# Three fixed buffers in place of a ring of three, earlier weight differences, and a third engine for sixteen weight products

## The chip, the cores and the metric

The kernel runs on one core of one Trainium2 chip. The metric is the device time of one execution in microseconds (us). The engines are named as the profile names them: PE (TensorE, matrix products), DVE (VectorE), ACT (ScalarE), POOL (GpSimd) and SP (SyncE). PSUM is the memory that PE writes its results to, SBUF the memory that the other operands lie in.

## What is computed

Sliding-window attention with four sink positions over 4 batches, 8 heads, 768 positions and head size 64, and behind it a layer norm and an MLP with a ReLU and a residual sum:

```
keep   = (key position < 4) or (0 <= query - key < 128)
a      = softmax(q k^T / 8 where keep, else -1e9)
x      = a v, heads side by side: (4, 768, 512)
xn     = (x - mean) / sqrt(var + 1e-6) * g_ln
out    = x + relu(xn @ w_ch1) @ w_ch2        # w_ch1 512 x 2048, w_ch2 2048 x 512
```

Inputs and output are float32; matrix operands are bfloat16.

## The kernel before

The 3072 rows are worked in 12 chunks c of 256 rows, two tiles t of 128 rows each; three chunks make a batch. Each chunk has an attention part (`attend_tile` for chunks 0 and 1, `attend` after them): scores on PE (L732), their exponentials on ACT (L746), a product with the mask on DVE (L750), and the product with v on PE (L769, L774). `value` then makes the row of x on DVE (L787 reciprocal, L789 x, L793 and L795 the norm's statistics), 1/sqrt(var) on POOL (L801, L802) and the centred row xc on DVE (L804). Each chunk has an MLP part (`mlp`): eight products with w1 (named ph, L839 for chunks 0 and 1 and L846 after them), eight ReLUs (named rl, L856 on ACT or L858 on DVE), and the product with w2. For chunks 0 and 1 that second product is the plain one (L877, L885). From chunk 2 on it is Strassen's (Winograd's form): `wino` makes sums of the hidden blocks (s1 to s4, L909, DVE) and seven products (p1 to p7, L926), some of them with four differences of blocks of w2, t1 to t4, which are made once (the lines named w2t, L997). DVE adds the results (L940, L947).

The norm's gain g_ln is folded into the activations for chunks 0 to 2. For chunk 3 and later it is multiplied into w1 once, in place: sixteen products of 128x512 with a column of g_ln (named w1g, L987 to L990). The four that belong to one quarter of w1 can start when chunk 2 has made its last use of that quarter, and chunk 3 needs them.

Nothing is ordered by hand. Every operation is entered with the engines it may run on and their planned costs (time on the engine, time to the result), what it depends on, and a priority. `Plan.run` lays them out in planned time: an operation takes the engine that would end it first, and of those that could start within a quarter of a microsecond, the one with the lowest priority number goes first. PE operations of priority 40 and more keep strict priority order. The resulting order is what each engine's queue gets, and each engine then works through its queue in that order.

The first q and k rows (chunk 0's first tile, as float32) and the q and k of chunks 1, 2 and 3 come through a ring `n4` of three buffers; after them the buffers are used for t1, t2 and t3, and t4 has a tile of its own. The loads of w2 are POOL DMAs (L523).

```
    ring("n4", 3, [128, H, 4, 64], BF16)
    n4_b = [Buf(f"n4_{c}", "n4") for c in range(1, PAR["by_dma"])]
    idle = [o for z in n4_b for o in z.users]
```

`idle` holds every user of the buffers of chunks 1, 2 and 3, and each of the sixteen differences waits for all of them.

Of the kernel before, what the change touches and what calls it, by code (L numbers as in the profile page):

```python
# [7 lines left out]
FP32 = mybir.dt.float32  # L8
BF16 = mybir.dt.bfloat16
# [192 lines left out]
def act(n):  # L202
    t = 0.065 + 0.000833 * n
    return (t, t + 0.105)
# [7 lines left out]
def fix(occ, extra=0.09):  # L212
    return (occ, occ + extra)
# [4 lines left out]
SW_4 = (1.4, 0.7, 0.9)  # L218
# [10 lines left out]
PAR = dict(strict=40.0, win=0.4, tr=-8.0, sc=-5.3, sc1=-2.0, av=2.0, trx=9.0, by_dma=4, x_by_dma=3,  # L229
           w1p=(1.6, 2.6, 2.7, 2.8), pm=2, w2p=(4.5, 4.51, 4.52, 4.53), by_tile=2, wino=2, vp=(0.0, 0.1, 2.0, 2.1, 4.2, 4.3), ld1=0.05)  # L230


def general(tc, nc, slots, pairs, ones, ident_f, ident, w1, w2, mhalf, g_s, g_r, q, k, v, out, scale):


    V, A, G, T, DMA = nc.vector, nc.scalar, nc.gpsimd, nc.tensor, nc.gpsimd.dma_start
    B, H, S, D = q.shape
    RB, HP, NS, DM = S // 128, H // 2, g_s.shape[2], H * D
    f32 = {n: [t.bitcast(FP32) for t in slots[n]] for n in ("kq", "n4", "kts", "pe")}
    flat = lambda t: t.rearrange("p a b -> p (a b)")  # L240
    half = [t.rearrange("p a k b -> p (a k b)")[:, 512 * i:512 * i + 512] for t in f32["kq"] for i in range(2)]
    q_n, k_n, v_n = half[0], half[1], half[2:4]
    qT, kT0, kT1 = [t.rearrange("p (a b) -> p a b", a=HP) for t in half[4:7]]
    kT, ksT = [kT0, kT1], f32["kts"][0]
    ks_n, vs_n = flat(f32["pe"][6]), flat(f32["pe"][7])
    sc = [f32["n4"][i].rearrange("p h i d -> p (h i d)").rearrange("p (h c) -> p h c", h=4) for i in range(2)]
    aT = [[flat(f32["pe"][2 * i + a]) for a in range(2)] for i in range(3)]
    xs, os_, xn, xnt = slots["ot"][0:2], slots["ot"][2:4], slots["xc"][0], slots["xnt"][0]
    h1 = [slots["hq"][u // 4][:, u % 4, :] for u in range(8)]
# [7 lines left out]
    with tc.For_i(0, B, 1) as b:  # L257
# [5 lines left out]
        for r in range(RB):  # L263
            x, cur, prev = xs[r % 2], r % 2, (r + 1) % 2
# [67 lines left out]
            st = slots["st"][r % 2]  # L332
# [5 lines left out]
            pb = ones[0].bitcast(BF16)  # L338
# [23 lines left out]
def kernel(  # L362
# [12 lines left out]
    nc = tc.nc  # L375

    B, H, S, D = q.shape
# [17 lines left out]
    P = Plan()  # L395

    def ring(name, n, shape, dtype, pool=consts):
        P.ring(name, [Slot(pool.tile(shape, dtype, name=f"{name}{i}"), f"{name}{i}") for i in range(n)])
# [3 lines left out]
    ones = [psum.tile([128, 512], FP32, name=f"one{i}") for i in range(4)]  # L402
    P.ring("pair", [Slot(pairs[i], f"pair{i}", banks[2 * i:2 * i + 2]) for i in range(2)])
    P.ring("one", [Slot(ones[i], f"one{i}", [banks[4 + i]]) for i in range(4)])
    ring("n4", 3, [128, H, 4, 64], BF16)
    ring("nat", 8, [128, H, 64], BF16)
    ring("vn", 7, [128, H, 65], BF16)
    ring("kq", 4, [128, HP, 2, 256], BF16)
# [12 lines left out]
    def const(name, shape, dtype):  # L421
        return consts.tile(shape, dtype, name=name)

    ident_f, ident = const("ident_f", [128, 128], FP32), const("ident", [128, 128], BF16)
# [7 lines left out]
    w1 = [const(f"w1_{c}", [128, NDM, 512], BF16) for c in range(4)]  # L432
    w2 = [const(f"w2_{c}", [128, 4, DM], BF16) for c in range(4)]
    w2t = [t.rearrange("p (c s n) -> p c s n", c=4, s=2) for t in (
        *[z.tile.rearrange("p h i d -> p (h i d)") for z in P.rings["n4"]], const("w2t", [128, 2048], BF16))]
    junk = const("junk", [128, 512], BF16)
    rec, low = const("rec", [128, NT, H], FP32), const("low", [128, NT, H], FP32)
    n_bad, flag = const("n_bad", [128, 1], FP32), const("flag", [1, 1], mybir.dt.int32)
# [9 lines left out]
    Bw2t = [[Buf(f"w2t{i}_{c}") for c in range(4)] for i in range(4)]  # L448
# [4 lines left out]
    V, G = nc.vector, nc.gpsimd  # L453
# [35 lines left out]
    def negs(e):  # L489
# [15 lines left out]
         writes=[Bc["gt"]], dma=HW_T)  # L505
    for h in range(H):
        p0 = 32 * (h // 2) + NS * (h % 2)
# [14 lines left out]
    for c in range(4):  # L522
        P.op(f"w2ld{c}", {"POOL": (0.75, 0.8)}, PAR["w2p"][c], lambda e, c=c: G.dma_start(  # L523
            w2[c], moe_w_ch2[512 * c:512 * (c + 1), :].rearrange("(t p) n -> p t n", p=128)),
            writes=[Bw2[c]], dma=SW_W)
# [7 lines left out]
    xnt_t = [Buf(f"xnt_t{t}") for t in range(NT)]  # L533

    tile_of, scores = {}, {}
    n4_b = [Buf(f"n4_{c}", "n4") for c in range(1, PAR["by_dma"])]

    def early(t):
        return 0.5 + 0.8 * t
# [22 lines left out]
    def load4(c, nm, prio, loaded):  # L562
        b, R = c // RC, c % RC
        p0 = 64 * "kq".index(nm)
        ap = (k if nm == "k" else q)[b, :, 256 * R:256 * R + 256, :].rearrange("h (p i) d -> p h (i d)", i=4)
        P.op(f"{nm}ld{c}", {"POOL": (0.72, 0.75)}, prio, lambda e: G.dma_start(
            n4_b[c - 1].t[p0:p0 + 64].rearrange("p h i d -> p h (i d)"), ap), writes=[loaded, n4_b[c - 1]], dma=SW_4)

    def chunk(c):
        b, R = c // RC, c % RC  # L570
        d = at(c, "tr") if c >= 2 else early(2 * c)
        ld = d - 14.0 if c >= RC else 4.0
        T = Buf(f"kq{c}", "kq")
        kq_b[c] = T
        if c == 0:
            f0, c0 = Buf("f0", "n4"), Buf("c0", "hq")
            raw = lambda: f0.t.rearrange("p h i d -> p (h i d)").bitcast(FP32).rearrange("p (h i d) -> p h i d", h=H, i=2)
            cut = lambda: c0.t.rearrange("p a b -> p (a b)")[:, 0:1024].rearrange("p (i h d) -> p i h d", i=2, h=H)
            for x, src in enumerate((k, q)):
                ap = src[b, :, 0:128, :].rearrange("h (p i) d -> p h (i d)", i=2)  # L580
# [4 lines left out]
            for x, (nm, src) in enumerate((("k", k), ("q", q))):  # L585
                nat.append(Buf(f"{nm}n01", "nat"))
                ap = src[b, :, 128:256, :].rearrange("h p d -> p h d")
                P.op(f"{nm}ld01", {"POOL": (0.87, 0.9)}, -50 + 0.1 * x, lambda e, nat=nat[x], ap=ap: G.dma_start(nat.t, ap),  # L588
                     writes=[nat[x]], dma=SW)
            for t in range(2):  # L590
                for hh in range(2):
                    hs = slice(4 * hh, 4 * hh + 4)
                    pt, done, half = Buf(f"pt0{t}{hh}", "one"), Buf(f"T0{t}{hh}"), Buf(f"c0{hh}")
# [6 lines left out]
                    def tr(e, pt=pt, t=t, hh=hh):  # L600
                        pb = pt.t.bitcast(BF16)[:, 0:512]
                        for h in range(2):
# [7 lines left out]
                         hold=[T] + ([] if t else [c0]), writes=[pt])  # L610
# [5 lines left out]
        elif c < PAR["by_dma"]:  # L616
            loaded = Buf(f"l{c}")
            for i in range(2):
                load4(c, "kq"[i], (PAR["ld1"] if c == 1 else ld) + 0.01 * i, loaded)
            for hh in range(2):  # L620
                pt = Buf(f"pt{c}{hh}", "one")

                def tr(e, pt=pt, hh=hh):
                    pb = pt.t.bitcast(BF16).rearrange("p (h k i g) -> p h i k g", h=2, k=2, i=4)
                    for h in range(2):
                        for i in range(4):
                            for h2 in range(2):
                                nc.tensor.transpose(pb[64 * h2:64 * h2 + 64, h, i], n4_b[c - 1].t[:, 4 * hh + 2 * h + h2, i, :], ident)  # L628
                P.op(f"tr{c}{hh}", pe(0.46), d + 0.02 + 0.1 * hh, tr, reads=[loaded, Bc["ident"]],
                                  hold=[n4_b[c - 1], T], writes=[pt], mode="c")  # L630
                done = Buf(f"T{c}{hh}")
                tile_of[2 * c, hh] = tile_of[2 * c + 1, hh] = done
                evict(f"ev{c}{hh}", d + 0.05 + 0.1 * hh, 1024,
                      lambda pt=pt: pt.t.bitcast(BF16).rearrange("p (m i g) -> p m g i", m=4, i=4),
                      lambda hh=hh: T.t[:, 2 * hh:2 * hh + 2].rearrange("p h k (g i) -> p (h k) g i", i=4), [pt], [T, done], fp=True)
        else:
            for x, (nm, src) in enumerate((("k", k), ("q", q))):
                for i in range(2):
                    nat = Buf(f"{nm}n{c}{i}", "nat")
                    ap = src[b, :, 256 * R + 128 * i:256 * R + 128 * (i + 1), :].rearrange("h p d -> p h d")  # L640
                    P.op(f"{nm}ld{c}{i}", {"POOL": (0.87, 0.9)}, ld + 0.01 * i + 0.1 * x,
                         lambda e, nat=nat, ap=ap: G.dma_start(nat.t, ap), writes=[nat], dma=SW, after=behind(c))  # L642
                    P.op(f"tr{nm}{c}{i}", {"SP": (1.2, 1.2)}, d + 0.01 * i, lambda e, nat=nat, i=i, x=x: dma_t(
                        T.t[:, :, x, 128 * i:128 * i + 128], nat.t.rearrange("p h d -> p (h d)")),
                        reads=[nat], writes=[T], dma=HW_X, after=[scores[c - 1]])
        if R == 0:
            kts = Buf(f"kts{b}", "kts")
# [334 lines left out]
    for c in range(NC):  # L982
        mlp(c)
        if c == PAR["x_by_dma"] - 1:
            for s in range(4):
                for j in range(NDM):
                    P.op(f"w1g{s}{j}", {"DVE": fix(0.36), "ACT": act(512)}, 16.0 * c + 11.0 + 2 * s + 0.1 * j,  # L987
                         lambda e, s=s, j=j: (V.tensor_scalar_mul if e == "DVE" else nc.scalar.mul)(  # L988
                             w1[s][:, j, :], w1[s][:, j, :], gt[:, j:j + 1]),
                         reads=[Bw1[s], Bc["gt"]], writes=[Bw1g[s]], after=last_use[s])  # L990

    idle = [o for z in n4_b for o in z.users]
    for qt in range(4):
        b11, b12, b21, b22 = (w2[qt][:, 2 * i:2 * i + 2, 256 * j:256 * j + 256] for i in range(2) for j in range(2))
        t1, t2, t3, t4 = (w2t[i][:, qt] for i in range(4))
        for i, (o, x0, x1) in enumerate(((t1, b12, b11), (t2, b22, t1), (t3, b22, b12), (t4, b21, t2))):
            P.op(f"w2t{i}_{qt}", {"DVE": dve(512, 0.52)}, 16.0 * PAR["wino"] - 6.0 + qt + 0.1 * i, lambda e, o=o, x0=x0, x1=x1: V.tensor_tensor(  # L997
                o, x0, x1, op=ALU.subtract), reads=[Bw2[qt]] + ([Bw2t[i - 1][qt]] if i in (1,) else [Bw2t[1][qt]] if i == 3 else []),
                writes=[Bw2t[i][qt]], after=idle)

    def guard(e):
        V.tensor_scalar(low, rec, LOW, HIGH, op0=ALU.max, op1=ALU.min)
# [12 lines left out]
    t, was = 1.3, "n"  # L1015
    for o in order:
# [7 lines left out]
        if free and left > 0.11:  # L1024
            i, nth = min(free)[1], 0
# [6 lines left out]
        t, was = o.start + o.engs["PE"][0], o.mode_out  # L1032
# [6 lines left out]
                o.emit(o.eng)  # L1039
    bad = nc.values_load(flag, min_val=0, max_val=128 * NT * H)  # L1040
    with tc.If(bad > 0):
        slots = {n: [s.tile for s in P.rings[n]] for n in ("kq", "kts", "n4", "pe", "ot", "xc", "xnt", "hq", "st")}
        general(tc, nc, slots, pairs, ones, ident_f, ident, w1, w2, mhalf, g_s, g_r, q, k, v, out, scale)
    global LAST
    LAST = P
# [35 lines left out]
```

## Time and profile before

| | us |
|---|---|
| median of 3 runs | 217.86 (217.83 to 217.99) |
| profiled execution, its own time | 217.35 |
| its span in the trace | 215.9 |
| PE busy, matmuls | 206.2 (96%) |
| DVE busy | 159.9 (74%) |
| ACT busy | 118.1 (55%) |
| POOL busy | 84.1 (39%) |
| granted TensorE clock, mean | 0.998 |

A profile row names the line, the engine, the operation, output and input by their names in the program with the buffer number left out (so n4, kq or w2t appear as n, kq or w2t, and w1 and w2 both as w). A stretch "idle before" an instruction is put down to whatever released it last. The end of a matmul is modelled, so that consecutive matmul groups overlap a little in the timeline.

### The profile page before, as it was taken

How to read it: one execution, taken by the hardware profiler on the slowest of the kernel's cores; microseconds unless marked ns; L12 is line 12 of the kernel's file. 1: busy time of each engine (PE TensorE's matmuls, PEld its weight loads, DVE VectorE, ACT ScalarE, POOL GpSimd, SP SyncE). 2: the span in 40 equal slices, each digit the busy share in tenths (PEclk: the TensorE clock that was granted, in tenths of full speed). 3: DMA queues.
4: the chain of work that ended last, by engine and by line, in shares of the span. 5: the costliest groups of instructions: out<-in, count | busy, mean ns of one | idle time of the engine just before them, and what ended most of it. 6: DMA issues, size and time to landing. Idle time of an engine off the chain costs nothing.

```text
span 215.9 us, 5921 instructions
## 1 busy us (share of the span) xinstructions
PE 206.2 (96%) x2381; PEld 168.5 (78%) x2387; DVE 159.9 (74%) x402; ACT 118.1 (55%) x182; POOL 84.1 (39%) x126
## 2 busy tenths in 40 slices
PE   6989999999998999999999999999999999999990
PEld 2568995684785897897987987988988988988880
DVE  5499644598898689699687796797786787794470
ACT  2578567166799655554556456455456456432600
POOL 7968574487057048048066075075110110110000
PEclk9999999999999999999999999999999999999999
DMA  6999999999929949949949959929942520222003
GB/s 109 169 185 207 193 197 206 179 203 157 191 51 136 155 100 110 164 123 114 179 100 148 195 56 150 210 34 155 170 104 37 149 49 0 100 49 99 2 3 109
DMA packets 100146, 27.23 MB, mean 126 GB/s; under 512 B 88848, under 2 KB 97040, under 8 KB 100112
## 3 DMA queue, kind: packets, MB, share of 16 engines
q0 software_dynamic: 67712, 13.37, 79.3%
q1 hardware_dynamic: 31872, 13.15, 31.5%
q8 instruction: 20, 0.33, 0.6%
q10 hardware_dynamic: 528, 0.26, 0.5%
q14 instruction: 14, 0.11, 0.2%
HBM read 27.30 MB, written 6.29 MB: 156 GB/s over the span
## 4 chain that ended last, share of the span: by engine, by line
PE 81%; ACT 6%; POOL 4%; DMA 3%; DVE 1%; issue 1%; DVEq 0%; ACTq 0%; POOLq 0%
PE one L846 30%; PE one L926 27%; PE one L839 6%; PE one L877 5%; PE pair L732 4%; PE pair L774 4%; ACT w L988 4%; DMA n<-in_q_dram 3%; PE pair L769 2%; POOL nat L642 2%; PE one L628 1%; POOL nat L588 1%; ACT pe L746 1%; ACT hq L856 1%; PE one L812 1%
## 5 line engine op out<-in xcount | busy, mean ns | idle before, releaser
L856 ACT ACTIVATE hq<-one 128x512 bf16<-128x512 f32 x93 | 55.5, 597 | 56.6 <-PE one L846 44.6
L846 PE MATMUL one<-xnt,w 128*128 128x256 bf16 x640 | 74.4, 273 | 0.0
L846 PEld LDWEIGHTS <-w 128*128 128x128 bf16 x640 | 61.4, 98 | 7.1
L746 ACT ACTIVATE pe<-pair 128x1024 bf16<-128x1024 f32 (+1 forms) x40 | 36.3, 957 | 22.4 <-PE pair L732 21.0
L801 POOL TENSOR_SCALAR st<-st 128x1 f32<-128x1 f32 x24 | 6.6, 274 | 92.6 <-DVE rec L787 77.0
L926 PEld LDWEIGHTS <-hs 128*128 128x128 bf16 x320 | 30.0, 98 | 5.6 <-issue 1.3
L926 PE MATMUL one<-n,hs 128*128 128x256 bf16 x240 | 29.6, 273 | 0.0
L750 DVE TENSOR_TENSOR pe<-pe,mask 128x1024 bf16<-128x1024 bf16 (+1 forms) x40 | 24.9, 644 | 5.0 <-ACT pe L746 4.9
L940 DVE TENSOR_TENSOR tm<-one,x 128x256 f32<-128x256 f32 x40 | 16.8, 421 | 12.2 <-PE one L926 12.1
L926 PEld LDWEIGHTS <-hq 128*128 128x128 bf16 x240 | 23.3, 98 | 3.0 <-ACT hq L856 0.3
L553 POOL DMA_DIRECT2D vn<-in_v_dram x24 | 21.7, 922 | 3.0 <-PE one L877 0.9
L926 PE MATMUL one<-w,hq 128*128 128x256 bf16 x160 | 19.3, 273 | 0.0
L909 DVE TENSOR_TENSOR hs<-hq 128x512 bf16<-128x512 bf16 x40 | 15.4, 413 | 5.1 <-ACT hq L856 5.1
L947 DVE TENSOR_TENSOR ot<-one,tm 128x256 f32<-128x256 f32 x40 | 16.7, 417 | 1.3 <-PE one L926 1.1
L789 DVE TENSOR_TENSOR x<-pair,rec 128x512 bf16<-128x512 f32 x24 | 16.6, 691 | 0.8
L793 DVE BATCH_NORM_STATS2 st<-x 128x6 f32<-128x512 bf16 x24 | 16.6, 690 | 0.4
L839 PE MATMUL one<-xnt,w 128*128 128x128 bf16 x256 | 16.0, 219 | 0.0
L642 POOL DMA_DIRECT2D nat<-in_k_dram x16 | 14.9, 931 | 2.7 <-DMA w<-in_moe_w_ch_dram 2.7
L642 POOL DMA_DIRECT2D nat<-in_q_dram x16 | 14.2, 904 | 3.4 <-DMA w<-in_moe_w_ch_dram 3.4
L802 POOL TENSOR_TENSOR st<-st,mhalf 128x1 f32<-128x1 f32 x24 | 14.7, 612 | 2.0
L877 PE MATMUL one<-w,hq 128*128 128x512 bf16 x60 | 15.0, 380 | 0.2
L839 PEld LDWEIGHTS <-w 128*128 128x128 bf16 x256 | 14.6, 98 | 0.7
(94 smaller groups left out, 234.6 us busy)
## 6 DMA issues: line engine op xcount, KB each, us to landing
out_dram<-ot SPq DMA_DIRECT2D x24, 256.0 KB
w<-in_moe_w_ch_dram POOLq DMA_DIRECT2D x8, 512.0 KB, 13.3
vn<-in_v_dram POOLq DMA_DIRECT2D x24, 128.0 KB, 7.2
nat<-in_k_dram POOLq DMA_DIRECT2D x17, 128.0 KB, 5.4
nat<-in_q_dram POOLq DMA_DIRECT2D x17, 128.0 KB, 6.6
n<-in_k_dram POOLq DMA_DIRECT2D x3, 256.0 KB, 13.5
n<-in_q_dram POOLq DMA_DIRECT2D x3, 256.0 KB, 14.5
kq<-nat SPq DMA_TRANSPOSE x32
```

The costliest lines, as they stand in the source:

```text
L553: P.op(f"vld{t}", {"POOL": (0.87, 0.9)}, prio, lambda e: G.dma_start(bv.t[:, :, 0:64], v[b, :, 128 * r:128 * (r + 1), :].rearrange("h p d ...
L642: lambda e, nat=nat, ap=ap: G.dma_start(nat.t, ap), writes=[nat], dma=SW, after=behind(c))
L746: P.op(f"ex{c}{hp}", {"ACT": act(2 * n)}, d + 0.1 + 0.05 * j, lambda e, pp=pp, pb=pb: nc.scalar.activation(pb.t[:, :, 0:n], pp.t[:, :, 0:n ...
L750: V.tensor_mul(pb.t[:, :, 0:n], pb.t[:, :, 0:n], mm),
L789: P.op(f"x{t}", {"DVE": dve(512)}, d + 0.11, lambda e: V.tensor_tensor(x.t.rearrange("p (a h c) -> p a h c", a=2, c=64), pv()[:, :, :, 0:6 ...
L839: nc.tensor.matmul(ph.t[:, 128 * s:128 * s + 128], lhsT=w1[u // 2][:, j, 128 * s:128 * s + 128], rhs=xnt.t[:, j, 128 * (u % 2):128 * (u % ...
L846: nc.tensor.matmul(ph.t[:, 256 * s:256 * s + 256], lhsT=w1[ht // 4][:, j, 128 * (ht % 4):128 * (ht % 4 + 1)], rhs=xnt.t[:, j, :], start=j ...
L856: nc.scalar.activation(hg.t[:, u % 4, :], ph.t, AF.Relu)
L877: nc.tensor.matmul(pc.t[:, 0:wd], lhsT=(hq[s // 2].t[:, (2 * s + i) % 4, 128 * ii:128 * ii + 128] if by_tile else hq[ht // 8].t[:, ht // 2 ...
L926: nc.tensor.matmul(at(r), lhsT=get(left, g)[:, v, s, :], rhs=rhs, start=first and n == 0, stop=n == 7, skip_group_check=True)
L940: return P.op(f"tm{name}_{c}", {"DVE": dve(256, 1.14)}, pr, lambda e: V.tensor_tensor(tm[name].t, at(r), xs[i].t[:, sl], op=ALU.add), read ...
L947: return P.op(f"o{c}_{half}", {"DVE": dve(256, 1.14)}, pr, lambda e: V.tensor_tensor(ots[i].t[:, sl], at(r), tm[name].t, op=ALU.add), read ...
```

## The change

There are three parts. The ring of three becomes three rings of one buffer, n4a, n4b, n4c, and the loads are tied to them: chunks 0 and 3 in n4a, chunk 1 in n4b, chunk 2 in n4c. The first load, a buffer of its own name before, is the first of the same list. Second, each of the four differences waits only for the users of the buffer that it is written to: t1 goes to n4b, t2 to n4c, t3 to n4a, and t4, in its own tile, waits for no buffer. Third, the sixteen products of w1 with the gain may also run on POOL, at a planned 0.9 us on the engine and 1.0 us to the result, and their planned cost on ACT goes from 0.49 and 0.60 us to 0.61 and 0.72 us.

```diff
-    ring("n4", 3, [128, H, 4, 64], BF16)
+    for i in range(3):
+        ring(f"n4{'abc'[i]}", 1, [128, H, 4, 64], BF16)
...
-        *[z.tile.rearrange("p h i d -> p (h i d)") for z in P.rings["n4"]], const("w2t", [128, 2048], BF16))]
+        *[P.rings[f"n4{x}"][0].tile.rearrange("p h i d -> p (h i d)") for x in "bca"], const("w2t", [128, 2048], BF16))]
...
-    n4_b = [Buf(f"n4_{c}", "n4") for c in range(1, PAR["by_dma"])]
+    n4_b = [Buf(f"n4_{c}", f"n4{'abca'[c]}") for c in range(PAR["by_dma"])]
...
-            n4_b[c - 1].t[p0:p0 + 64].rearrange("p h i d -> p h (i d)"), ap), writes=[loaded, n4_b[c - 1]], dma=SW_4)
+            n4_b[c].t[p0:p0 + 64].rearrange("p h i d -> p h (i d)"), ap), writes=[loaded, n4_b[c]], dma=SW_4)
...
-            f0, c0 = Buf("f0", "n4"), Buf("c0", "hq")
+            f0, c0 = n4_b[0], Buf("c0", "hq")
...
-                    P.op(f"w1g{s}{j}", {"DVE": fix(0.36), "ACT": act(512)}, 16.0 * c + 11.0 + 2 * s + 0.1 * j,
-                         lambda e, s=s, j=j: (V.tensor_scalar_mul if e == "DVE" else nc.scalar.mul)(
+                    P.op(f"w1g{s}{j}", {"DVE": fix(0.36), "ACT": (0.61, 0.72), "POOL": (0.9, 1.0)}, 16.0 * c + 11.0 + 2 * s + 0.1 * j,
+                         lambda e, s=s, j=j: (nc.scalar.mul if e == "ACT" else V.tensor_scalar_mul if e == "DVE" else G.tensor_scalar_mul)(
...
-    idle = [o for z in n4_b for o in z.users]
+    idle = [[o for z in n4_b if z.ring == f"n4{x}" for o in z.users] for x in "bca"] + [[]]
...
-                writes=[Bw2t[i][qt]], after=idle)
+                writes=[Bw2t[i][qt]], after=idle[i])
```

The remaining lines of the diff give the same three buffers their new names where the general path (L233, run only if a softmax sum is out of bounds) uses them.

More of the change, by code (lines that the diff above doesn't have):

```diff
@@ L238, in general @@
     RB, HP, NS, DM = S // 128, H // 2, g_s.shape[2], H * D
-    f32 = {n: [t.bitcast(FP32) for t in slots[n]] for n in ("kq", "n4", "kts", "pe")}
+    f32 = {n: [t.bitcast(FP32) for t in slots[n]] for n in ("kq", "n4a", "n4b", "kts", "pe")}
     flat = lambda t: t.rearrange("p a b -> p (a b)")
@@ L245, in general @@
     ks_n, vs_n = flat(f32["pe"][6]), flat(f32["pe"][7])
-    sc = [f32["n4"][i].rearrange("p h i d -> p (h i d)").rearrange("p (h c) -> p h c", h=4) for i in range(2)]
+    sc = [f32[("n4a", "n4b")[i]][0].rearrange("p h i d -> p (h i d)").rearrange("p (h c) -> p h c", h=4) for i in range(2)]
     aT = [[flat(f32["pe"][2 * i + a]) for a in range(2)] for i in range(3)]
@@ L627, in tr @@
                             for h2 in range(2):
-                                nc.tensor.transpose(pb[64 * h2:64 * h2 + 64, h, i], n4_b[c - 1].t[:, 4 * hh + 2 * h + h2, i, :], ident)
+                                nc.tensor.transpose(pb[64 * h2:64 * h2 + 64, h, i], n4_b[c].t[:, 4 * hh + 2 * h + h2, i, :], ident)
                 P.op(f"tr{c}{hh}", pe(0.46), d + 0.02 + 0.1 * hh, tr, reads=[loaded, Bc["ident"]],
-                                  hold=[n4_b[c - 1], T], writes=[pt], mode="c")
+                                  hold=[n4_b[c], T], writes=[pt], mode="c")
                 done = Buf(f"T{c}{hh}")
@@ L1041 @@
     with tc.If(bad > 0):
-        slots = {n: [s.tile for s in P.rings[n]] for n in ("kq", "kts", "n4", "pe", "ot", "xc", "xnt", "hq", "st")}
+        slots = {n: [s.tile for s in P.rings[n]] for n in ("kq", "kts", "n4a", "n4b", "pe", "ot", "xc", "xnt", "hq", "st")}
         general(tc, nc, slots, pairs, ones, ident_f, ident, w1, w2, mhalf, g_s, g_r, q, k, v, out, scale)
```

## The prediction

> **What bounds the kernel now.** The summary by engine comes first: PE is busy 206.2 of 215.9 us, and the row of granted clock is 9 in every slice, so a change of DVE, ACT and POOL work can move the end only where PE stands still for it. In the view by slices, PE stands at 9 from 16 us on in all slices but that of 64.8 to 70.2 us and the last. Next, busy time by stretches, for the MLP of chunk 2 (its ph products, then its Strassen products with the scores of chunk 4 among them) and, as a control, the same two stages of chunk 5, which issue the same PE work and have no w1g products:
>
> ```profile
> 55.44:63.17 7.73, 7.73 (x89) 7.00 (x88) 6.92 (x16) 6.38 (x12) 1.43 (x4) 1.00 0.75 139
> 63.17:72.47 9.30, 8.07 (x87) 6.23 (x85) 7.46 (x21) 9.25 (x14) 5.63 (x7) 1.00 1.45 111
> 104.12:111.85 7.73, 7.73 (x91) 6.99 (x89) 6.06 (x16) 4.18 (x7) 2.03 (x5) 1.00 1.65 163
> 111.85:119.50 7.65, 7.65 (x87) 6.18 (x85) 5.93 (x17) 4.69 (x6) 4.99 (x6) 1.00 1.49 122
> ```
>
> The columns are the stretch, its length, and the busy time of PE, PE's weight loads, DVE, ACT and POOL. The first stage is equally long in both chunks. The second takes 9.30 us against 7.65: **1.65 us lost**, with ACT busy for 9.25 of it. The chain that ended last says with what:
>
> ```profile
> 64.84 0.84 ACT w L988 x2
> 65.68 0.20 issue
> 65.89 0.02 ACTq L754
> 65.90 0.05 issue
> 65.96 1.95 ACT w L988 x3
> 67.91 0.91 ACT pe L746
> 68.81 0.61 ACT w L988
> 69.42 0.92 ACT pe L746
> 70.34 0.04 issue
> 70.38 0.40 PE pair L732 x6
> ```
>
> The w1g products (L988) stand before the exponentials (L746) of chunk 4, and PE cannot write its second half of scores until an exponential empties a pair of PSUM banks. The timeline and the waits show the loss at PE:
>
> ```profile
> 70.38 0.23 PE L732 MATMUL pair<-kq,kq 64*128 64x128 bf16 x2 [1.12 <-ACT pe L746]
> PEld L926 <- ACT hq L856: 0.3, 1, 0.3
> ```
>
> That is 1.12 us there and 0.3 us where p2 waits for the last ReLU; the other 0.2 us are smaller gaps. The differences of w2 lie elsewhere: sixteen L997, starting between 46.87 and 53.21 us. PE in 44 to 56 us is busy 3.95, 3.89 and 3.95 of 4 us each, so it loses 0.21 us there in all.
>
> **The change, part by part.** *Buffers.* In the ring, three loads take the three buffers, and the fourth (chunk 3, issued at 27.68) can take the first load's, which its casts at 6.7 us had freed long before. That is the new assignment too. No operation is added or removed, and POOL's and SP's DMAs stay as they were: 0.
>
> *Differences.* t1, t2 and t4 no longer wait for chunk 3's transposes (L628, 45.69 to 46.7), only for the w2 quarter and for transposes that ended by 30.4. POOL's queue shows when w2 lands, since its DMAs wait for it:
>
> ```profile
> 32.53 0.88 POOL L642 DMA_DIRECT2D nat<-in_k_dram  x1 [1.29 <-DMA w<-in_moe_w_ch_dram]
> 34.81 0.87 POOL L642 DMA_DIRECT2D nat<-in_k_dram  x1 [1.40 <-DMA w<-in_moe_w_ch_dram]
> 37.35 0.87 POOL L642 DMA_DIRECT2D nat<-in_q_dram  x1 [1.67 <-DMA w<-in_moe_w_ch_dram]
> 39.95 0.87 POOL L642 DMA_DIRECT2D nat<-in_q_dram  x1 [1.72 <-DMA w<-in_moe_w_ch_dram]
> ```
>
> L997 starts every 0.37 us (0.33 to 0.45), so three differences per landing are 1.1 us, twelve 4.4 us. DVE is busy 5.11 us of 30 to 40 and 2.28 of 40 to 44, so 6.6 us are free. The first thing behind them on DVE's in-order queue is the mask product of chunk 2 (last one 38.17 to 38.86); PE reads it at 40.89, which leaves 2.0 us. So three differences ahead of it, and a landing that comes up to 0.9 us after its planned place, cost nothing; beyond that PE pays one for one. The last three end about 41.1, before the reciprocal at 41.58. What leaves 46.87 to 53.2 frees DVE where PE lost 0.21 us. Bounds: 0.2 us gained, 0.5 us lost if PE's order (free below priority 40) comes out worse. I take 0, the nearest row being PE's own 99%.
>
> *Products.* Before, 14 ran on ACT, two on DVE. ACT's 14 start 0.61 us apart when back to back (five in 64.73 to 67.9). The planner gives POOL a product whenever ACT is booked more than 0.28 us ahead (1.0 less 0.72). POOL is free from 57.2 to about 65.3 but for two 1/sqrt pairs (0.83 us planned, 0.87 measured): (8.1 - 1.7)/0.9 = 7 products. So 7 on POOL, 7 on ACT, two on DVE. ACT sheds 7 x 0.61 = 4.3 us. Its last ReLU then ends near 63.95, two products follow until 65.2, and the control puts the first exponential 2.27 us after the ph products, here at 65.44: in time. The 1.12 us stall goes, with the small gaps. Of p2's 0.3 us I keep 0.2, since the control has the ReLU end exactly when p2 starts, and a product may stand half in the way. ACT's gain: 1.65 - 0.2 = 1.45 us.
>
> What a POOL product takes no row shows. Below: a 128x1 TENSOR_SCALAR takes 0.22 us, a 128x128 select 0.29, hence 0.22 + 511 x 0.07/127 = 0.50. Above: the dearest fixed cost, 0.57 (L802, 128x1), plus ACT's 0.72 for the same product, 1.3. I take 0.9, the middle. The Trainium skill (GPSIMD Engine Reference, Performance versus the Vector engine) has 769 ns for 512 elements in a tight loop; no run here shows it, and seven by that are 0.9 us less on POOL, with the sum unchanged.
>
> **What speaks against it** is a row from the start of the kernel, where both engines read SBUF at once:
>
> ```profile
> 18.93 0.68 DVE L692 TENSOR_TENSOR pe<-pe,mask 128x1024 bf16<-128x1024 bf16 x1
> 18.97 1.07 POOL L802 TENSOR_TENSOR st<-st,mhalf 128x1 f32<-128x1 f32 x1
> ```
>
> L802 takes 0.57 us alone and 1.07 here: it waited out DVE's instruction. L801 likewise goes from 0.22 to 0.37 beside an xc (L804). Nothing here shows DVE waiting for POOL, because POOL's instructions are short and DVE waits for their results anyway. The Trainium skill (SBUF — State Buffer, SBUF: two separate sides) says that the port pair is an exclusive lock for the whole instruction, whichever engine starts first, for DVE instructions with two SBUF inputs or a two-port mode. The trace agrees for POOL waiting (0.5 us); by the rule for both directions the gain would be 0.45 (217.4), with POOL alone waiting 1.45 (216.4).
>
> The mechanism, from rows: POOL goes from each 1/sqrt pair straight to a product, and DVE's xc (L804, behind that pair) and its eight sums (L909) come into up to five products. If each holds DVE for half its length, that is 5 x 0.45 = 2.25 us; if for all, 4.5; if DVE does not wait, 0. In the control the sum that p6 needs ends at 114.09 and p6 starts at 115.33: 1.24 us of slack. PE would thus lose 0, 1.0 or 3.3 us of its 1.45. I take 0.5, between none and the half.
>
> Sum: 1.45 - 0.5 = 0.95, with 0 from the differences. Against the profiled execution: span 215.9 - 0.95 = 214.95, plus the 1.45 us outside the span (217.35 - 215.9), 216.4. That execution was 0.5 us under the median of the runs, so **216.9** against the median 217.86.
>
> **The rivals.** (1) *DVE is held up by POOL and becomes the bound, slower.* Place: p7 and p6 of chunk 2. It decides from 1.24 + 1.45 = 2.7 us of DVE delay; at 3.6 (0.72 per meeting) it is 217.86 + 0.9 = 218.8, at the full 4.5 219.7. For it: DVE is busy 6.92 and 7.46 us in the two stages, 2.4 more than in the control, and the row above. Against: two L858 ReLUs (0.68 each) and two L988 (0.34) make up 2.0 of that 2.4 and can go to a lighter ACT. A POOL product of 1.3 us or more leads to the same place, the xc behind it coming late. (2) *The gain is eaten, no change:* the same, with 2.2 to 3.1 us of delay (1.45 us less a stall within 0.44 of it), 217.4 to 218.3. (3) *The planner gives POOL few products*, since ACT and DVE end each sooner: with three, ACT sheds 1.8 us, enough for the 1.12 us stall alone, and 3 x 0.45 us of DVE delay cost 0.1: 216.8, inside the forecast. (4) *A difference blocks DVE while its w2 quarter is under way*, and chunk 2's attention is late: with more than 2.0 us of it PE loses the excess; 1 us more gives 217.9 after the gain.
>
> **How the numbers follow.** About 0.2% (0.44 us) can be told from no change. Gain of more than that, by the forecast or (3): 0.58, spanning 216.2 (1.65 us, all of it) to 217.4. Rival (2) 0.14 and (4) 0.05 give no change: 0.19. Rival (1) 0.18, and PE's order worse by more than 0.5 us in 32 to 56 us 0.05: slower, 0.23. The range goes from 216.1 to 218.6; under it 0.05, over it 0.10. The forecast's own range is 216.2 to 217.4.
>
> **What would show it.** Right: L997 twelve times between 32 and 42 us and four times after 46.7; about seven POOL rows L988 of 0.5 to 1.3 us between 57 and 66; the second stage of chunk 2 at 7.7 to 8.6 us instead of 9.30; no PE wait for an L746 there. Wrong: PE waiting for L909 at p7 or p6, L804 or L909 starting late behind an L988 of POOL, a stage of 9.3 us or more, or PE under 3.85 of 4 us anywhere in 32 to 56.

## The result and the profile after

The changed kernel takes 218.63 us (median of 16 runs, 217.9 to 219.74) against 217.85 us before (16 runs, 217.07 to 218.34): a ratio of 1.0047, 95% interval 1.0031 to 1.0063. The medians differ by 0.78 us and the means by 1.03; the interval of the ratio spans 0.7 to 1.4 us. The kernel is slower by about half a per cent, where the forecast was 0.95 us faster, with a chance of 0.23 for slower. The median lies 0.03 us above the predicted range.

The profiled execution of the changed kernel took 219.26 us, span 217.8. That is 1.9 us more than the profiled execution of before, and not all of it is the change. Line numbers are one higher than before from the ring's definition on. The program is the same up to the first landing of w2, yet PE reaches chunk 1's transposes (L629) at 13.46 us here and at 12.68 before, because chunk 1's q rows landed later. Over all the profiles below that moment lies anywhere from 12.09 to 13.62 us, whatever the kernel. That would account for the spread of the times of one kernel, more than a microsecond (it is not shown, as each kernel has one profile). It is the reason why stages are compared below and not ends.

Three stages tell the change. Their limits are PE's first instruction of each: chunk 3's transposes, chunk 2's first ph product, its product p1, chunk 3's first ph product. Busy time by these stretches, with the columns as in the prediction (length, then PE, weight loads, DVE, ACT, POOL); the first row is the first stage before, the other three are the changed kernel's:

```profile
45.69:55.44 9.75, 9.53 (x88) 4.80 (x89) 8.95 (x26) 7.70 (x15) 6.70 (x9) 1.00 2.37 183
...
46.56:56.96 10.40, 9.63 (x90) 4.79 (x89) 6.95 (x19) 7.70 (x15) 6.81 (x9) 1.00 1.84 183
56.96:64.69 7.73, 7.73 (x89) 6.99 (x88) 5.49 (x11) 6.22 (x11) 5.87 (x6) 1.00 0.55 100
64.69:74.44 9.75, 8.16 (x86) 5.99 (x84) 8.15 (x23) 7.81 (x12) 7.33 (x9) 1.00 1.15 103
```

Before, the first of them took 9.75 us, the second 7.73, the third 9.30 (the prediction shows the rows of these two). So there are **two separate losses, 0.65 us in the first stage and 0.45 us in the third**, 1.10 us together. All other stages agree within 0.1 us. The timelines show who waited in the first stage, before (two lines) and in the changed kernel:

```profile
49.55 0.47 POOL L801 TENSOR_SCALAR st<-st 128x1 f32<-128x1 f32 x1
...
51.21 0.40 PE L812 MATMUL one<-ident,xc 128*128 128x128 bf16 x4
...
48.67 0.63 POOL L802 TENSOR_SCALAR st<-st 128x1 f32<-128x1 f32 x1
49.39 0.57 POOL L803 TENSOR_TENSOR st<-st,mhalf 128x1 f32<-128x1 f32 x1
...
49.99 0.41 DVE L805 TENSOR_SCALAR xc<-x,st 128x512 bf16<-128x512 bf16 x1 [0.77 <-POOL st L803]
...
50.46 0.40 PE L813 MATMUL one<-ident,xc 128*128 128x128 bf16 x4 [0.77 <-DVE xc L805]
```

PE stands for 0.77 us before the transposes of tile 5, waiting for DVE's xc, which waits for POOL's 1/sqrt; before, it didn't wait there. And in the third, again first two lines of before, the xc of the two tiles:

```profile
60.53 0.41 DVE L804 TENSOR_SCALAR xc<-x,st 128x512 bf16<-128x512 bf16 x1 [0.19 <-POOL st L802]
63.44 0.41 DVE L804 TENSOR_SCALAR xc<-x,st 128x512 bf16<-128x512 bf16 x1 [0.17 <-POOL st L802]
...
58.66 3.14 POOL L989 TENSOR_SCALAR w<-w,gt 128x512 bf16<-128x512 bf16 x2 [5.13 <-PE one L847]
61.88 0.22 POOL L802 TENSOR_SCALAR st<-st 128x1 f32<-128x1 f32 x1
62.76 3.11 POOL L989 TENSOR_SCALAR w<-w,gt 128x512 bf16<-128x512 bf16 x2
65.95 0.22 POOL L802 TENSOR_SCALAR st<-st 128x1 f32<-128x1 f32 x1
...
62.79 0.79 DVE L805 TENSOR_SCALAR xc<-x,st 128x512 bf16<-128x512 bf16 x1 [0.93 <-POOL st L803]
66.86 0.41 DVE L805 TENSOR_SCALAR xc<-x,st 128x512 bf16<-128x512 bf16 x1 [0.95 <-POOL st L803]
...
65.97 1.26 PE L927 MATMUL one<-w,hq 128*128 128x256 bf16 x10 [0.46 <-DVE hq L859]
69.25 0.61 PE L927 MATMUL one<-n4a,hs 128*128 128x256 bf16 x4 [0.71 <-DVE hs L910]
71.17 1.03 PE L927 MATMUL one<-w2t,hq 128*128 128x256 bf16 x8 [0.43 <-DVE tm L941]
```

A w1g product takes POOL 1.57 us. Four of them, two ahead of each 1/sqrt pair, make each xc wait almost a microsecond (0.19 and 0.17 before), everything behind xc on DVE is late, and PE waits for DVE three times. The 1.12 us wait for ACT's exponential is gone, as forecast; the waits for DVE are more.

### The profile page after: what moved, and what is told of

It reads as the page before. It is cut to its first block, busy times and chain, and to the rows that moved or that the text cites. A ratio compares the mean times of both kernels' runs of the same rounds, so it can differ in the third digit from the quotient of the medians.

```text
span 217.8 us, 5925 instructions
## 1 busy us (share of the span) xinstructions
PE 206.8 (95%) x2387; PEld 168.0 (77%) x2387; DVE 161.1 (74%) x401; ACT 116.6 (54%) x179; POOL 90.0 (41%) x130
## 4 chain that ended last, share of the span: by engine, by line
PE 79%; DVE 9%; POOL 4%; DMA 4%; issue 1%; DVEq 0%; POOLq 0%
PE one L847 30%; PE one L927 27%; PE one L878 6%; PE one L840 5%; PE pair L733 4%; PE pair L775 4%; DMA n4b<-in_q_dram 4%; DVE st L794 2%; PE pair L770 1%; DVE x L790 1%; DVE hs L910 1%; POOL st L803 1%; PE one L629 1%; POOL nat L589 1%; POOL nat L643 1%
## 5 line engine op out<-in xcount | busy, mean ns | idle before, releaser
L878 PE MATMUL one<-w,hq 128*128 128x512 bf16 x64 | 15.3, 380 | 0.0
L803 POOL TENSOR_TENSOR st<-st,mhalf 128x1 f32<-128x1 f32 x24 | 14.2, 591 | 2.0
L805 DVE TENSOR_SCALAR xc<-x,st 128x512 bf16<-128x512 bf16 x24 | 10.2, 425 | 6.3 <-POOL st L803 6.2
```

The costliest lines, as they stand in the source:

```text
L878: nc.tensor.matmul(pc.t[:, 0:wd], lhsT=(hq[s // 2].t[:, (2 * s + i) % 4, 128 * ii:128 * ii + 128] if by_tile else hq[ht // 8].t[:, ht // 2 ...
```

## The experiments

The first two runs take the parts of the change one by one, the next two take the first loss apart. Lengths are those of the three stages, in order, from one profile each.

**The early differences alone.** The third part of the change is undone:

```diff
-    {"DVE": fix(0.36), "ACT": (0.61, 0.72), "POOL": (0.9, 1.0)}
+    {"DVE": fix(0.36), "ACT": act(512)}
```

> The changed kernel without its third part: the sixteen w1g products keep the costs and engines of before, the differences of w2 stay early. Theory: the change loses in two separate places, and this kernel has the first alone. From chunk 3's transposes to chunk 2's first ph product PE takes 10.4 us as in the changed kernel (9.75 before), because PE's queue has the transposes of tile 5 earlier than xc can deliver them; the second Strassen stage of chunk 2 takes 9.3 us as before. Together 217.85 + 0.65 = 218.5. Rival: the early differences cost nothing, all the loss comes from POOL's products: 9.75 and 9.3 us, 217.85.

Measured: 10.41, 7.73 and 9.30 us; 218.19 against 217.57, ratio 1.0032 (1.0015 to 1.0049). The first loss is that of the differences alone, with the same 0.77 us wait.

**POOL's share alone.**

```diff
-                writes=[Bw2t[i][qt]], after=idle[i])
+                writes=[Bw2t[i][qt]], after=[o for z in idle for o in z])
```

> The changed kernel with all sixteen differences waiting for all three buffers again, as before; POOL keeps its share of the w1g products. Theory: only the second place is left. 9.75 us from chunk 3's transposes to the first ph product, then 9.7 us for the Strassen stage of chunk 2, since POOL's products of 1.57 us stand ahead of its 1/sqrt pairs and DVE's xc waits: 217.85 + 0.45 = 218.3. Rival (the stage is worse only because the earlier loss shifts it, and POOL's share helps by itself): 8.5 us and 217.0.

Measured: 9.76, 7.73 and 9.76 us; 218.06 against 217.57, ratio 1.0021 (1.0006 to 1.0036). The second loss is that of POOL's share alone. By stages the two losses add up to the change's.

**The place of tile 5's transposes in PE's queue.**

```diff
-             hold=[xnt_b[c]])
+             hold=[xnt_b[c]], nb=49.6 if t == 5 else 0.0)
```

> The changed kernel, with the transposes of tile 5 not planned before 49.6 us, so that PE's queue has them behind one more product with w2, where they stood before. Everything else, the early differences too, stays. Theory: the first loss is the place of these transposes in PE's queue, so PE takes 9.75 us there again, and only the second loss is left: 218.3. Rival: the loss is DVE being late with the differences or with xc whatever PE's order: 10.2 us or more, 218.7 or more.

Measured: 9.47, 7.72 and 9.75 us; 217.65 against 217.57, ratio 1.0002 (0.9983 to 1.0022). With PE's order of before, the early differences lose nothing; they gain 0.28 us, more than the 0.21 us that the prediction had counted as PE's idle time there, and more than the theory said. So the place of the transposes in PE's queue makes the first loss. How they came there can be read from the queues. Of DVE's sixteen differences nine are made between 33 and 42 us, and only one is left in front of tile 5's aggregate (L796), where six were. It starts 1.50 us after the start of chunk 3's transposes (3.43 before). The planner puts the 1/sqrt pair after two of POOL's four loads instead of after all four, and then places the transposes of tile 5 in PE's queue four matmuls L878 behind those of tile 4, where before twelve and eight matmuls of chunk 3's scores lay between. On the chip xc comes later than these transposes' turn, and PE, in order, stands still.

**Why xc is later than planned.** In the kernel with the early differences alone, the three differences that DVE makes back to back at that moment are left out, with every order kept:

```diff
-    lambda e, o=o, x0=x0, x1=x1: V.tensor_tensor(
+    lambda e, o=o, x0=x0, x1=x1, out=(i, qt) in ((2, 1), (2, 2), (0, 3)): None if out else V.tensor_tensor(
```

> The kernel with the early differences alone (w1g as before), and the three differences that DVE makes back to back while POOL makes tile 5's 1/sqrt left out (t3 of quarters 1 and 2, t1 of quarter 3 keep what lay there). Orders as planned with them. Theory: those three hold POOL's first instruction of the pair back, so it drops from 0.63 to 0.22 us, xc comes 0.4 us sooner, PE's wait before tile 5's transposes falls from 0.77 to about 0.35 us and the stage from chunk 3's transposes to the first ph product from 10.4 to 10.0 us. Rival (POOL is late only by its DMA issues): 0.77 and 10.4 us stay.

Measured: 10.00, 7.72 and 9.30 us (one execution). The timeline of this kernel:

```profile
46.47 1.86 POOL L643 DMA_DIRECT2D nat<-in_k_dram  x2
48.41 0.22 POOL L802 TENSOR_SCALAR st<-st 128x1 f32<-128x1 f32 x1
...
49.78 0.40 PE L813 MATMUL one<-ident,xc 128*128 128x128 bf16 x4 [0.35 <-DVE xc L805]
```

POOL's first instruction takes 0.22 instead of 0.63 us and PE's wait drops from 0.77 to 0.35, both as expected. So 0.4 us of the wait is POOL held back by DVE's differences. The rest has no run of its own, but the row of POOL's two loads fits it: the aggregate was done at 47.98 us, the loads that stand ahead of the 1/sqrt pair at 48.33, 0.35 us later.

**Half a product.** POOL makes 256 of 512 columns:

```diff
-    w1[s][:, j, :], w1[s][:, j, :], gt[:, j:j + 1]),
+    w1[s][:, j, 0:256 if e == "POOL" else 512], w1[s][:, j, 0:256 if e == "POOL" else 512], gt[:, j:j + 1]),
```

> The changed kernel, but where POOL makes a w1g product it makes only the first 256 of the 512 columns (the other half keeps w1 without the gain). Same order on every engine. Theory: a POOL product is too long for the gap it was planned into; at half the columns it takes about 0.8 us, the 1/sqrt pairs are not held up, and the Strassen stage of chunk 2 drops from 9.75 to 8.3 us or less; with the first loss kept, 217.85 + 0.65 - 1.0 = 217.5. Rival (POOL and DVE shut each other out at SBUF, whatever the length): DVE's sums and xc still run late, 9.3 us or more, 218.5. If most of the 1.57 us is fixed cost, the product stays above 1.2 us and the stage near 9.5.

Measured: 10.42, 7.73 and 8.01 us; 216.96 against 217.57, ratio 0.9968 (0.9951 to 0.9984). The order on every engine is that of the changed kernel; only the four POOL instructions are shorter, and the third stage falls by 1.74 us. The row of this kernel:

```profile
L989 POOL TENSOR_SCALAR w<-w,gt x4: 915/934/946, 56.7 to 61.9; 128x256 bf16<-128x256 bf16 x4
```

With 1.57 us for 512 columns, that makes 2.5 ns a column and 0.29 us fixed, if the time is linear between these two. At 0.93 us the 1/sqrt pairs are no longer held up: xc waits 0.19 and 0.17 us, as before. Had a whole product taken the 0.9 us that the plan and the prediction gave it, the third stage would by this have been near 8 us.

**The cost put right.** POOL's planned cost becomes the measured one:

```diff
-    {"DVE": fix(0.36), "ACT": (0.61, 0.72), "POOL": (0.9, 1.0)}
+    {"DVE": fix(0.36), "ACT": (0.61, 0.72), "POOL": (1.57, 1.65)}
```

> The changed kernel, with POOL's planned cost of a w1g product set to what the trace shows, 1.57 us (0.9 in the change). The plan then gives POOL two products instead of four and none of them is planned across a 1/sqrt pair. Theory: the first loss stays, 10.4 us from chunk 3's transposes on; xc waits only for the half microsecond that a product holds DVE off, and the Strassen stage of chunk 2 takes 8.4 us instead of 9.75: 217.5 + 0.65 - 0.9 = 217.3. Rival (any product on POOL costs as much as it saves): 9.3 us, 218.1.

Measured: 10.41, 7.73 and 8.60 us; 217.66 against 217.59, ratio 1.0001 (0.9982 to 1.002). Two products go to POOL, and no xc waits longer for its 1/sqrt than before. The third stage gains 0.70 us on before, the first loses 0.66: no change in the sum. That is 0.4 us above what I expected, and the third stage is still 0.95 us over the control's 7.65. One xc that starts 0.03 us after a product takes 0.79 instead of 0.41 us. The other takes 0.78 beside POOL's loads and no product. That isn't alone: beside a load of v rows near 17 us, an xc takes 0.45 to 0.78 us in 13 of the 14 profiles (0.35 in that of before), and late_prio_cost and best below each have a w1g product on DVE that takes 0.70 or 0.71 beside such a load. So loads of POOL's seem to hold such an instruction up as well; no run tried it.

**Behind the 1/sqrt pairs.** To keep POOL's products clear of them, the last quarter's four go to POOL alone, planned at 1.57 us (differences as before):

```diff
-    {"DVE": fix(0.36), "ACT": (0.61, 0.72), "POOL": (0.9, 1.0)}
+    {"POOL": (1.57, 1.65)} if s == 3 else {"DVE": fix(0.36), "ACT": (0.61, 0.72)}
```

> The differences wait as before. The four w1g products of the last quarter of w1 go to POOL alone, at a planned 1.57 us, and no other; the rest to ACT (0.61) and DVE. POOL's queue then has the same number of products, four, but behind both 1/sqrt pairs, beside DVE's sums for chunk 2's Strassen products. Theory (what cost time was a long product ahead of the 1/sqrt pairs in POOL's queue): chunk 2's Strassen stage takes 8.0 us, the time is about 1.2 us below before, 216.4. Rival (DVE's sums, with two SBUF inputs each, are shut out while POOL works): sums of 0.8 us and more instead of 0.42, the stage at 9.3 us or more, 217.6 or more.

Measured: 9.76, 7.72 and 10.41 us; 219.24 against 217.4, ratio 1.0087 (1.0061 to 1.0112). My theory fails here: with no product ahead of a 1/sqrt pair, this is the worst of all. But the plan had also put four w1g products of DVE's own in front of the second half of the sums, so two causes were mixed. (The stage accounts for 1.11 of the 1.84 us between the medians; the one profile is of the second shortest of six runs, and what the others lost more isn't known.) The next pair parts them: late priorities, the differences as before, ACT alone for twelve products, and POOL's four made in one kernel and left out in the other.

```diff
-    {"DVE": fix(0.36), "ACT": (0.61, 0.72), "POOL": (0.9, 1.0)}, 16.0 * c + 11.0 + 2 * s + 0.1 * j,
+    {"POOL": (1.57, 1.65)} if s == 3 else {"ACT": (0.61, 0.72)}, 16.0 * c + 21.5 + 0.5 * s + 0.1 * j,
```

> Late priorities, differences as before, twelve w1g products on ACT alone, the last four on POOL alone, behind both 1/sqrt pairs and beside DVE's sums; no w1g product on DVE. Theory (a product of POOL holds DVE's SBUF-reading instructions off during its first 0.8 to 1.0 us, and lets them through after that): each of the three products beside the sums costs one DVE instruction 0.4 to 0.75 us, some 1.5 us, against 1.2 us of slack: sums of up to 1.2 us in the trace, the Strassen stage of chunk 2 at 8.0 to 8.5 us. Rival (DVE was late in the kernel with a tail of four only because it had three w1g products of its own in front of the sums): 7.7 us, as without POOL.

> The kernel with the tail of four on POOL, late priorities and ACT for the rest, but with POOL's four products left out (the last quarter of w1 keeps no gain); every other instruction and order is the same. Theory: all sums of DVE at 0.42 us, the Strassen stage of chunk 2 at 7.7 us. What the run with the four products takes more than this one is the price of POOL working beside DVE. Rival (no contention): the same stage in both.

Measured: third stage 8.70 us with POOL's products, 7.65 us without (one execution each; first stage 9.76 and 9.75). The timeline with them:

```profile
64.51 6.30 POOL L989 TENSOR_SCALAR w<-w,gt 128x512 bf16<-128x512 bf16 x4
...
64.33 1.16 DVE L910 TENSOR_TENSOR hs<-hs,hq 128x512 bf16<-128x512 bf16 x1
65.52 0.43 DVE L910 TENSOR_TENSOR hs<-hq,hs 128x512 bf16<-128x512 bf16 x1
66.20 1.19 DVE L910 TENSOR_TENSOR hs<-hq 128x512 bf16<-128x512 bf16 x2
67.88 0.79 DVE L910 TENSOR_TENSOR hs<-hq,hs 128x512 bf16<-128x512 bf16 x1
69.27 1.22 DVE L751 TENSOR_TENSOR pe<-pe,mask 128x1024 bf16<-128x1024 bf16 x1
```

and without:

```profile
64.30 0.43 DVE L910 TENSOR_TENSOR hs<-hs,hq 128x512 bf16<-128x512 bf16 x1
64.76 0.43 DVE L910 TENSOR_TENSOR hs<-hq,hs 128x512 bf16<-128x512 bf16 x1
65.44 0.75 DVE L910 TENSOR_TENSOR hs<-hq 128x512 bf16<-128x512 bf16 x2
66.68 0.43 DVE L910 TENSOR_TENSOR hs<-hq,hs 128x512 bf16<-128x512 bf16 x1
67.97 0.68 DVE L751 TENSOR_TENSOR pe<-pe,mask 128x1024 bf16<-128x1024 bf16 x1
```

Each of the four products holds one DVE instruction up, by 0.73, 0.44, 0.36 and 0.54 us. So DVE does wait for POOL, and four products beside DVE's sums cost 1.05 us of PE's time. DVE's second instruction in a product, 65.52 to 65.95, runs at full speed while the first product goes on to about 66.1. So both mechanisms exist: a product standing in front of the 1/sqrt pair, and a product holding a DVE instruction up. In the changed kernel itself the second counts for little: of the 1.9 us by which its DVE falls behind, 0.74 and 0.78 are the longer waits for the 1/sqrt pairs and 0.38 is the one xc held up by a product.

**Another way to the same 1.65 us.** The kernel before, with the w1g products moved behind the exponentials in priority, and then also with ACT's measured cost:

```diff
-    {"DVE": fix(0.36), "ACT": act(512)}, 16.0 * c + 11.0 + 2 * s + 0.1 * j,
+    {"DVE": fix(0.36), "ACT": act(512)}, 16.0 * c + 21.5 + 0.5 * s + 0.1 * j,
...
+    {"DVE": fix(0.36), "ACT": (0.61, 0.72)}, 16.0 * c + 21.5 + 0.5 * s + 0.1 * j,
```

> The kernel before with one number changed: the priorities of the w1g products are moved behind those of chunk 4's exponentials (from 43 to 49.3 to 53.5 to 55.3), engines and costs as before. No POOL. Theory: the 1.65 us of before are exponentials and a ReLU queued behind w1g products on ACT; with two products fewer ahead of the exponentials the 1.12 us wait of PE goes, the late ReLU stays: stage 8.2 us, 216.5. Rival (ACT has too much to do there in any order): 9.0 us or more, 217.3 or more.

> As the one before it, and the planner is given ACT's measured cost of a w1g product, 0.61 and 0.72 us (0.49 and 0.60 before). Theory: the plan then no longer puts a product where the last ReLU has to go, and p2 does not wait either: stage 7.8 us, 216.0. Rival: the plan shifts ReLUs to DVE and p7 or p6 wait there: 8.5 us, 216.8.

Measured: third stage 8.08 us, 216.21 against 217.4, ratio 0.995 (0.9933 to 0.9968); with the cost as well 7.77 us, 216.34, ratio 0.9951 (0.9936 to 0.9966). In the first, ACT makes 14 products as before, so 1.22 of the 1.65 us go by order alone; in the second it makes twelve and DVE four, and 1.53 go. The 0.3 us between the two stages is not to be seen in the times. The prediction's reading of where the kernel before lost 1.65 us holds.

**Put together.** The early differences, the held transposes, the late priorities and ACT's cost, without POOL:

```diff
-    {"DVE": fix(0.36), "ACT": (0.61, 0.72), "POOL": (0.9, 1.0)}, 16.0 * c + 11.0 + 2 * s + 0.1 * j,
+    {"DVE": fix(0.36), "ACT": (0.61, 0.72)}, 16.0 * c + 21.5 + 0.5 * s + 0.1 * j,
...
-             hold=[xnt_b[c]])
+             hold=[xnt_b[c]], nb=49.6 if t == 5 else 0.0)
```

> The early differences of the changed kernel, the transposes of tile 5 held to 49.6 us in the plan, the late priorities and ACT's measured cost for the w1g products, and no POOL. Theory: the two stages add up from the runs that show them: 9.47 us from chunk 3's transposes to the first ph product (9.75 before) and 7.8 us for the Strassen stage (9.30 before), 217.57 - 0.28 - 1.5 = 215.8. Rival: the earlier first stage only brings the next wait forward, 216.1 or more.

Measured: 215.6 against 217.4, ratio 0.9915 (0.9901 to 0.9929), the fastest of all. Its first and third stage (the second is 7.73 us again):

```profile
46.06:55.53 9.47, 9.37 (x88) 4.89 (x89) 7.47 (x20) 6.57 (x11) 6.83 (x9) 1.00 1.98 181
...
63.26:71.04 7.78, 7.78 (x86) 6.17 (x84) 7.38 (x19) 7.78 (x12) 4.89 (x6) 1.00 1.54 125
```

0.28 and 1.52 us less than before make 1.80, the difference of the medians.

## Why the prediction was wrong, step by step

*What bounds the kernel.* Right. PE is the bound, the 1.65 us lost in chunk 2's Strassen stage lay in ACT's queue, and two experiments got 1.22 and 1.53 us of it back without touching POOL.

*Buffers: 0.* Right. Stage lengths up to chunk 3's transposes agree within 0.1 us but for the landing of the first rows.

*Differences: "I take 0, the nearest row being PE's own 99%".* This step failed first: 0.65 us, beyond its bound of 0.5 us lost. What I had looked at held: the differences fit into DVE's free time between 33 and 42 us, and chunk 2's attention was not late; DVE waited 0.72 us for one landing, covered by its slack. Nine came early and not twelve; what the three late ones cost was not tried, but one of them (t1 of the last quarter) is among the three that held POOL back. What I didn't follow was the order that this work had been part of: with most differences gone from 47 to 53 us, tile 5's statistics, POOL's pair and PE's transposes were planned earlier in three in-order queues. I had named "PE's order (free below priority 40)" and then priced it from a row that shows the old order. The row that bears on it was in the profile of before: POOL's 1/sqrt of tile 5 ran beside back-to-back L997 and took 0.47 instead of 0.22 us, and the whole pair 1.15 us (49.55 to 50.70) against 0.83 planned, so the chip was later than the plan there already.

*Products: "I take 0.9, the middle".* This failed second and most. The upper bound of 1.3 us was a small POOL instruction's time plus ACT's time for the product; the product took 1.57. The lower bound, from 0.07 us for 127 more columns of a select, had 0.55 ns a column against 2.5 measured. The figure of the Trainium skill (GPSIMD Engine Reference, Performance versus the Vector engine), 769 ns for 512 elements in a tight loop, is its best case, and half of this instruction's 1.57 us. "7 products" were four: I counted POOL's time as if ACT were always booked ahead, though I had named in rival (3) that ACT and DVE take a product whenever they end it sooner, and I counted as free until 65.3 us a POOL whose loads (L642) start at 63.36 before. ACT kept eleven.

*"What speaks against it".* The direction was right and the mechanism half right. I let xc meet a product that starts right behind a 1/sqrt pair; that happened once and cost 0.38 us. What cost most was the plainer thing that I gave half a sentence in rival (1): a product of 1.3 us or more standing in front of the pair in POOL's queue. The forecast's 0.5 us for PE's waiting on DVE was 1.60 us in three waits. The 1.24 us of DVE slack was mis-sized too. It was read from the control, whose DVE has less to do. In chunk 2 itself, before the change, the sum that the second half of p7 waits for ended at 66.03 us and PE took it at 66.44: 0.41 us of slack. In the changed kernel that sum comes 1.65 us later after p1's start, and PE, held up earlier in the stage already, waits 0.71 for it.

*The rule.* The Trainium skill (SBUF — State Buffer, SBUF: two separate sides) has the loser blocked for the whole instruction, and either engine able to lose. The runs agree that both lose: POOL 0.63 instead of 0.22 us, DVE up to 1.16 instead of 0.43. They don't agree on the whole instruction, as far as POOL's spans in a profile can be trusted (four products in a row in 6.30 us bear the 1.57 out): a sum held up by a product was done 0.98 us after the product's start at 64.51, and the next one ran at full speed with the product still going.

*The rivals.* Rival (1), slower by DVE as the bound, is what happened in the third stage, at 0.45 us instead of 0.9 or more; with the first stage's 0.65 us, for which the prediction had only the 0.05 of "PE's order worse by more than 0.5 us in 32 to 56 us", the sum came to its size by two halves. That 218.63 lies close to that rival's 218.8 is luck. Its chance of 0.18 was too low for a mechanism that needed only one unseen duration to be 0.27 us above the bound that I had guessed.

## What to carry to other kernels

When an engine takes over an instruction that it has never run in the trace, its duration is the whole question: run that instruction once before sharing work on it, and look first at what stands behind it in that engine's queue, since an instruction of 0.2 us can be the one that everything waits for. Taking work out of a planned order moves everything behind it: ask which in-order queue gets a later instruction put earlier, and how late the chip runs against the plan there. Where one engine holds up the bound by the order of its queue, change the order before moving the work: here one priority was worth more than a third engine.

## What the runs showed of the hardware

- A tensor_scalar on GpSimd with a per-partition scalar, bfloat16, in place, takes 1.57 us for 128x512 (1.55 to 1.58 in the changed kernel) and 0.93 us for 128x256. ACT does the 512 in 0.71 us, DVE in 0.34 when nothing holds it up.
- Such a product holds DVE's instructions up: one that meets its start ends 0.82 us (xc) to about 1.0 us (a sum) after that start, and a later sum in the same product takes its usual 0.43 us. Why DVE is let in before the product ends was not tried. The other way round, three differences on DVE stretch a 128x1 instruction of POOL's from 0.22 to 0.63 us.
- The landing of chunk 1's q rows, issued at 5.4 us, lets PE go on at 12.09 to 13.62 us, in 14 profiles whose programs are the same up to there.
